# Strided products of an attention kernel: which side of the multiplication takes the stride

## The chip, the cores and the metric

The kernel runs on one core of a Trainium2 chip. Its time is the device time of the whole program in microseconds (us), the median of several executions; lower is better. Beside the times there is a profile of one execution: every instruction of every engine with its start and duration.

The engines that matter here are TensorE (PE, matrix products into PSUM), VectorE (DVE, element by element), ScalarE (ACT, activation functions and copies) and the queues of GpSimd (POOL) and SyncE (SP), which issue the transfers. PSUM is the memory that TensorE writes, in eight banks; SBUF is the main memory on the chip. Both have 128 partitions, and an instruction runs over the same elements of many partitions at once.

## The reference

Sparse attention with 8 batches, 8 heads, 576 positions and 64 columns a head, then a layer with a squared ReLU:

```python
scores = scale * np.matmul(q, k.transpose(0, 1, 3, 2))
mask_local = (rel >= 0) & (rel < 32)
mask_strided = (rel >= 0) & (pos[None, :] % 32 == pos[:, None] % 32)
# heads 0 to 3: mask_local; heads 4 to 7: mask_strided; masked scores are -1e9
attn = softmax(scores)                     # float32, over the keys
x = concatenated heads of attn @ v         # (8 * 576, 512)
h = np.maximum(x @ w_in, 0.0)              # w_in (512, 2048)
out = (h * h) @ w_out                      # w_out (2048, 512)
```

In a head with the strided mask a position sees only positions with the same remainder modulo 32: 18 of the 576. The kernel keeps x transposed, as four tiles xt[0] to xt[3] of 128 partitions (two heads of 64 columns each) and 4608 columns (all positions of all batches), in bf16. The strided heads 4 to 7 are xt[2] and xt[3]. The 18 positions of one remainder stand 32 columns, 64 bytes, apart there.

## The kernel before

The order of all work is written out by hand. The layer runs in nine chunks of 512 positions. A chunk is 16 groups of mm1 (four matmuls against w_in, L744, one for each xt tile in the order 0 to 3; then a ReLU on ScalarE, L750, into one of four r buffers, and a square on VectorE, L754) and 16 groups of mm2 (four matmuls against w_out, L850). Only chunk 0 takes the xt tiles in another order (0, 2, 1, 3). The groups are numbered from 0, so chunk c starts at group 32 c. The last two chunks (SEVEN) use a scheme with seven products for mm2 (L820), for which VectorE prepares sums of weights (L775).

A table, PLAN, says which steps of the attention of later batches go in front of which group; BATCH0 orders the first batch before the first group. Each engine works through its instructions in this order, and waits where an operand isn't there or a buffer isn't free. Batch b has positions 576 b to 576 b + 575, so chunk 1 needs batch 1, chunk 2 batch 2, and so on; chunk 7 needs batches 6 and 7.

The strided heads of a batch from 1 on are done by step_SS (scores and exponentials) and step_XX (words x1.0, x1.1, x1.2 for the three parts of batch 1). They pack three heads of one remainder into a block of 3 x 18 = 54 columns, two remainders (par 0 and 1) on the lower and upper 64 partitions. A part has eight blocks; the third part has six, which hold the fourth head. In step_XX TensorE makes the sums of the exponentials (L622, bank pn) and the products with v (L625, bank po); ScalarE makes the reciprocal of the sums, rv, with a logarithm and an exponential (L627, L628); and VectorE multiplies po by rv into xt: L635 for the first two parts, six instructions of 144 elements each (8 blocks by 18 positions), and L641 for the third, for each par one of 270 elements (three groups of 5 blocks by 18) and one of 18 elements. The last L641 of a batch completes xt[3].

Batch 0 uses step_N and step_O with another layout: VectorE multiplies 576 elements at once on all 128 partitions (L672), once for xt[2] and once for xt[3].

PSUM banks go round in a list: after group 32 six banks rotate among step_SS, step_XX, the local heads' steps and step_G. step_G(b) makes the scores of all local heads of batch b (L587, 24 matmuls) and takes six banks at once; its 24 matmuls alternate between two rows of three banks, eight matmuls to each pair of banks.

Of the kernel before, what the change touches and what calls it, by code (L numbers as in the profile page):

```python
# [11 lines left out]
ALU = mybir.AluOpType  # L12
# [155 lines left out]
def kernel(  # L168
# [9 lines left out]
    nc = tc.nc  # L178
    B, H, S, D = q.shape
    d_model, d_ff = moe_w_in.shape  # L180
    T = B * S
    STRIDE = 32
    NA = S // STRIDE
# [3 lines left out]
    NJ = 8  # L187
    RH = STRIDE // NJ
    SP_ = RH * NA
# [4 lines left out]
    NG = 5  # L194
    NB = NP2 + NG + 1
    W3 = 3 * NA
# [27 lines left out]
    def bank(nm):  # L224
        if places:
            return all_banks[places.pop(0)]
        t = banks[nm].pop(0)
        banks[nm].append(t)
        while id(t) in unread:
            run_due(lambda x: x[1] == unread[id(t)])  # L230
        return t

    def bank_pair():

        i = places.pop(0)
        return all_banks[i:i + 2], psb[:, i:i + 2]
# [21 lines left out]
    xt = [singles.tile([128, T], BF16, name=f"xt{p}") for p in range(4)]  # L258
# [10 lines left out]
    rv0 = b0[:, n_s:n_s + 8 * S].bitcast(FP32).rearrange("p (u c) -> p u c", u=4)  # L269
# [204 lines left out]
    def run_due(test):  # L474
        due = [x for x in pending if test(x)]
        for x in due:
            pending.remove(x)
        for x in sorted(due, key=lambda x: x[0]):
            x[2]()
# [121 lines left out]
    def blocks(part):  # L601
        return range(NJ * part, min(NJ * (part + 1), NB))
# [14 lines left out]
    def step_XX(b, part):  # L617
        run_due(lambda x: x[1] == (b, part))
        vb, n = vbds[b % 2], len(blocks(part))
        e = es[2 + b % 2][:, NJ * W3 * part:NJ * W3 * part + W3 * n]  # L620
        pn, po = bank("pt")[:, 0:W3 * n], bank("pt")
        nc.tensor.matmul(pn, ones_bd, e, start=True, stop=True)  # L622
        for i, t in enumerate(blocks(part)):
            c = slice(W3 * i, W3 * (i + 1))
            nc.tensor.matmul(po[:, c], vb[:, t, :], e[:, c], start=True, stop=True)  # L625
        rv = rv_pool.tile([128, NJ * W3], FP32, name="rv")[:, 0:W3 * n]
        nc.scalar.activation(rv, pn, AF.Ln)  # L627
        nc.scalar.activation(rv, rv, AF.Exp, scale=-1.0)  # L628
        for h in (3,) if part == 2 else range(3):
            for par in range(2):  # L630
                r, x = slice(64 * par, 64 * par + 64), slice(64 * (h % 2), 64 * (h % 2) + 64)
                to = xt[2 + h // 2][x, b * S:(b + 1) * S].rearrange("c (m a r) -> c m a r", a=NP2, r=2)
                if part < 2:
                    of, by = (y[r, 0:W3 * n].rearrange("c (a h m) -> c h m a", a=n, h=3)[:, h] for y in (po, rv))
                    nc.vector.tensor_tensor(to[:, :, NJ * part:NJ * (part + 1), par], of, by, op=ALU.mult)  # L635
                    continue
                of, by = (y[r, 0:W3 * n].rearrange("c (a g m) -> c g m a", a=n, g=3) for y in (po, rv))
                for lo, g, k in ((0, 0, NG), (NG, 2, 1)):
                    t = to[:, :, 2 * NG * (g == 2) + lo, par]
                    t = bass.AP(t.tensor, t.offset, [t.ap[0], [2 * NG, 3 - g], [STRIDE, NA], [2, k]])  # L640
                    nc.vector.tensor_tensor(t, of[:, g:, :, lo:lo + k], by[:, g:, :, lo:lo + k], op=ALU.mult)  # L641

    def load_v0():
        load_v_local_sw(0)
# [17 lines left out]
    def step_O(u):  # L662
        s = st.pop(u)
        e, hw, w = s["e"], S // 2, SP_
        pos, both = bank_pair()
        for half, po in enumerate(pos):
            for t in range(hw // w):
                for h in range(2):
                    vt, c = vs0[:, u - 2, NJ * h + 2 * t + half], ER * half + hw * h + w * t
                    nc.tensor.matmul(po[64 * h:64 * h + 64, w * t:w * (t + 1)], vt, e[0:w, c:c + w],  # L670
                                     start=True, stop=True)
        nc.vector.tensor_tensor(  # L672
            xt[u][:, 0:S].rearrange("c (p j r) -> c p j r", j=NJ // 2, r=2),
            both[:, :, 0:hw].rearrange("c r (j p) -> c p j r", p=SP_),
            rv0[:, u].rearrange("c (r j p) -> c p j r", r=2, p=SP_), op=ALU.mult)

    def step_D0(u):
        s = st[u]
# [196 lines left out]
    def run_step(word):  # L875
# [18 lines left out]
        elif op == "N":  # L894
            step_N(int(arg))
        elif op == "O":
            step_O(int(arg))
        elif op in "sx":
            (step_SS if op == "s" else step_XX)(*(int(x) for x in arg.split(".")))
        elif op == "k":  # L900
            step_K(int(arg[0]), int(arg[1]), ENG[arg[2]])
# [145 lines left out]
    for line in PLAN.strip().splitlines():  # L1047
        n, words = line.split(":")
# [42 lines left out]
```

## Time and profile before

| | us |
|---|---|
| median of 3 runs | 301.19 |
| lowest and highest run | 297.56, 304.58 |
| the profiled execution | 296.99 |
| its span, first to last instruction | 295.2 |
| TensorE busy | 289.3 |
| VectorE busy | 220.0 |
| ScalarE busy | 170.7 |
| GpSimd busy | 82.7 |

A row of a group reads: line, engine, operation, output <- inputs, partitions x elements and type of the output <- of the inputs, xcount | busy us in total, mean ns of one | idle us of the engine just before them, and what ended most of it. A row of the chain that ended last reads: start us, us, engine, tile and line, count. A row of the timeline is the same with shapes, and in brackets the idle time before it and what ended it. A row of waits reads: who <- whom: us in total, times, longest us. L635 is line 635 of the kernel.

### The profile page before, as it was taken

How to read it: one execution, taken by the hardware profiler on the slowest of the kernel's cores; microseconds unless marked ns; L12 is line 12 of the kernel's file. 1: busy time of each engine (PE TensorE's matmuls, PEld its weight loads, DVE VectorE, ACT ScalarE, POOL GpSimd, SP SyncE). 2: the span in 40 equal slices, each digit the busy share in tenths (PEclk: the TensorE clock that was granted, in tenths of full speed). 3: DMA queues.
4: the chain of work that ended last, by engine and by line, in shares of the span. 5: the costliest groups of instructions: out<-in, count | busy, mean ns of one | idle time of the engine just before them, and what ended most of it. 6: DMA issues, size and time to landing. Idle time of an engine off the chain costs nothing.

```text
span 295.2 us, 5930 instructions
## 1 busy us (share of the span) xinstructions
PE 289.3 (98%) x2212; PEld 156.1 (53%) x2212; DVE 220.0 (75%) x553; ACT 170.7 (58%) x321; POOL 82.7 (28%) x123
## 2 busy tenths in 40 slices
PE   8989999999999999999999999999999999999995
PEld 3644555545545454554455445544454444894594
DVE  5657689697777759679367945786489989968983
ACT  3758846775668736774577447645665466307610
POOL 8974743004513054075104800000000013102300
PEclk9999999999999999999999999999999999999999
DMA  7999999999999899999988999411011110021003
GB/s 159 176 208 205 192 198 192 155 216 207 174 194 171 144 157 202 160 136 181 167 131 122 179 168 145 84 56 73 36 23 52 58 54 0 1 104 41 0 2 142
DMA packets 91724, 37.38 MB, mean 127 GB/s; under 512 B 77548, under 2 KB 85830, under 8 KB 91696
## 3 DMA queue, kind: packets, MB, share of 16 engines
q0 software_dynamic: 50608, 18.33, 55.6%
q1 hardware_dynamic: 40944, 18.62, 31.8%
q8 instruction: 17, 0.28, 0.4%
q14 instruction: 11, 0.09, 0.1%
q10 hardware_dynamic: 144, 0.07, 0.1%
HBM read 37.22 MB, written 9.44 MB: 158 GB/s over the span
## 4 chain that ended last, share of the span: by engine, by line
PE 97%; DVE 1%; ACT 0%; issue 0%; DVEq 0%
PE psb L744 42%; PE psb L850 33%; PE psb L820 9%; PE psb L703 2%; PE psb L867 2%; PE psb L625 1%; PE psb L611 1%; PE psb L490 1%; PE psb L542 1%; PE psb L622 1%; PE psb L587 1%; PE psb L512 1%; DVE xt L672 0%; PE psb L347 0%; PE psb L337 0%; DVE x_l L692 0%
## 5 line engine op out<-in xcount | busy, mean ns | idle before, releaser
L744 PE MATMUL psb<-xt,w_in_b 128*128 128x512 bf16 x576 | 133.4, 379 | 0.3 <-DVE xt L672 0.2
L750 ACT ACTIVATE r<-psb 128x512 bf16<-128x512 f32 x144 | 85.4, 599 | 47.6 <-PE psb L744 42.5
L850 PE MATMUL psb<-w_out_b,g_sb 128*128 128x512 bf16 x448 | 103.2, 379 | 0.0
L744 PEld LDWEIGHTS <-w_in_b 128*128 128x128 bf16 x576 | 53.1, 97 | 58.7 <-issue 1.4
L754 DVE TENSOR_TENSOR g_sb<-r 128x512 bf16<-128x512 bf16 x112 | 46.9, 423 | 34.9 <-ACT r L750 34.0
L850 PEld LDWEIGHTS <-g_sb 128*128 128x128 bf16 x448 | 41.0, 97 | 44.7 <-DVE g_sb L754 0.3
L635 DVE TENSOR_TENSOR xt<-psb,rv 64x144 bf16<-64x144 f32 x84 | 34.0, 405 | 10.1 <-ACT rv L628 9.0
L789 POOL CAST sa<-g_sb 128x256 fp32r<-128x256 bf16 x16 | 9.7, 608 | 100.9 <-DVE g_sb L784 100.9
L854 ACT COPY y<-psb 128x512 f32<-128x512 f32 x28 | 16.6, 591 | 29.4 <-PE psb L850 29.3
L627 ACT ACTIVATE rv<-psb 128x432 f32<-128x432 f32 (+1 forms) x21 | 10.5, 501 | 12.8 <-PE psb L622 12.8
L365 POOL DMA_DIRECT2D q_t<-in_q_dram x6 | 3.5, 578 | 45.9 <-DMA qT_s<-q_t 26.2
L709 DVE TENSOR_TENSOR x_l<-psb,rinv 96x384 bf16<-96x384 f32 x28 | 15.5, 554 | 1.0
L784 DVE TENSOR_TENSOR g_sb<-r 128x512 bf16<-128x512 bf16 x32 | 13.1, 420 | 2.4 <-ACT r L750 2.4
L598 ACT ACTIVATE e<-psb 128x384 bf16<-128x384 f32 x30 | 12.0, 513 | 4.2 <-PE psb L587 4.2
L612 ACT ACTIVATE e<-psb 128x432 bf16<-128x432 f32 (+1 forms) x21 | 10.4, 497 | 4.0 <-PE psb L611 4.0
L294 POOL DMA_DIRECT2D k_l<-in_k_dram x16 | 11.8, 742 | 1.8 <-DMA v_st<-in_v_dram 1.3
L820 PE MATMUL psb<-t,s 128*128 128x256 f32 x96 | 12.2, 283 | 0.0
L594 DVE TENSOR_TENSOR e<-e,mask_all 128x576 bf16<-128x576 bf16 x20 | 8.4, 456 | 5.1 <-ACT e L598 5.0
L641 DVE TENSOR_TENSOR xt<-psb,rv 64x270 bf16<-64x270 f32 (+1 forms) x28 | 11.0, 432 | 1.4 <-ACT rv L628 1.1
L294 POOL DMA_DIRECT2D q_l<-in_q_dram x16 | 11.6, 730 | 0.5 <-DMA k_l<-in_k_dram 0.5
L820 PEld LDWEIGHTS psb<-t,s 128*128 128x128 f32 x96 | 11.6, 189 | 0.0
L628 ACT ACTIVATE rv<-rv 128x432 f32<-128x432 f32 (+1 forms) x21 | 11.2, 533 | 0.7
(135 smaller groups left out, 313.5 us busy)
## 6 DMA issues: line engine op xcount, KB each, us to landing
out_dram<-y SPq DMA_DIRECT2D x35, 256.0 KB, 3.3
w_out_b<-in_moe_w_out_dram POOLq DMA_DIRECT2D x4, 512.0 KB, 15.4
q_t<-in_q_dram POOLq DMA_DIRECT2D x7, 288.0 KB, 7.2
k_t<-in_k_dram POOLq DMA_DIRECT2D x7, 288.0 KB, 6.8
vl<-in_v_dram POOLq DMA_DIRECT2D x6, 288.0 KB, 6.6
v_st<-in_v_dram POOLq DMA_DIRECT2D x7, 216.0 KB, 6.8
w_in_b<-in_moe_w_in_dram POOLq DMA_DIRECT2D x2, 704.0 KB, 13.9
k_l<-in_k_dram POOLq DMA_DIRECT2D x16, 72.0 KB, 7.4
```

What stands on the lines that cost most here:

```text
L294: nc.gpsimd.dma_start(out=t[:, :, hh, :], in_=src[b, 2 * p + hh].rearrange("(t p) d -> p t d", p=QL))
L598: nc.scalar.activation(e[:, row, 4 * QL * i:4 * QL * (i + 1)], bk[row][i][:, 0:4 * QL], AF.Exp, scale=scale)
L628: nc.scalar.activation(rv, rv, AF.Exp, scale=-1.0)
L635: nc.vector.tensor_tensor(to[:, :, NJ * part:NJ * (part + 1), par], of, by, op=ALU.mult)
L709: nc.vector.tensor_tensor(x, po[0:QL, :, 0:D], rinv[0:QL].to_broadcast([QL, NL, D]), op=ALU.mult)
L744: nc.tensor.matmul(ph, w_in_b[:, kk, 128 * ff:128 * (ff + 1)], xt[kk][:, 512 * c:512 * (c + 1)], start=(kk == order[0]), stop=(kk == order ...
L750: nc.scalar.activation(r, ph, AF.Relu)
L754: later(1, lambda: nc.vector.tensor_tensor(g[:, ff, :], r, r, op=ALU.mult))
L784: nc.vector.tensor_tensor(g[:, ff, :], r, r, op=ALU.mult)
L820: nc.tensor.matmul(pa, a, b, start=k == 0 and n not in "273", stop=k == 7, skip_group_check=True)
L850: nc.tensor.matmul(py, g[:, ff, 128 * j:128 * (j + 1)], w_out_b[:, ff, :], start=(ff == 0), stop=(ff == 15))
L854: nc.scalar.copy(y, py)
```

## The change

All three products multiply two operands that lie packed (the positions of one remainder are neighbours) into an output in which they are apart. An instruction walks its operands and its output in one common order. Before, the order is that of the output: the inner loop goes over neighbouring remainders in xt and steps through both inputs by 54 floats (L635, L641), or by 72 and by half a buffer (L672). After, the order is that of the inputs: the inner loop goes over 18 (or 72) neighbours in po and rv, and steps through xt by 32 columns (L635, L641) or by 8 (L672). The elements, their number, the types, the instructions and their places in the order stay.

```diff
@@ step_XX
                 if part < 2:
-                    of, by = (y[r, 0:W3 * n].rearrange("c (a h m) -> c h m a", a=n, h=3)[:, h] for y in (po, rv))
-                    nc.vector.tensor_tensor(to[:, :, NJ * part:NJ * (part + 1), par], of, by, op=ALU.mult)
+                    of, by = (y[r, 0:W3 * n].rearrange("c (a h m) -> c h a m", a=n, h=3)[:, h] for y in (po, rv))
+                    t = to[:, :, NJ * part:NJ * (part + 1), par].rearrange("c m a -> c a m")
+                    nc.vector.tensor_tensor(t, of, by, op=ALU.mult)
                     continue
-                of, by = (y[r, 0:W3 * n].rearrange("c (a g m) -> c g m a", a=n, g=3) for y in (po, rv))
+                of, by = (y[r, 0:W3 * n].rearrange("c (a g m) -> c g a m", a=n, g=3) for y in (po, rv))
                 for lo, g, k in ((0, 0, NG), (NG, 2, 1)):
                     t = to[:, :, 2 * NG * (g == 2) + lo, par]
-                    t = bass.AP(t.tensor, t.offset, [t.ap[0], [2 * NG, 3 - g], [STRIDE, NA], [2, k]])
-                    nc.vector.tensor_tensor(t, of[:, g:, :, lo:lo + k], by[:, g:, :, lo:lo + k], op=ALU.mult)
+                    t = bass.AP(t.tensor, t.offset, [t.ap[0], [2 * NG, 3 - g], [2, k], [STRIDE, NA]])
+                    nc.vector.tensor_tensor(t, of[:, g:, lo:lo + k], by[:, g:, lo:lo + k], op=ALU.mult)
@@ step_O
         nc.vector.tensor_tensor(
-            xt[u][:, 0:S].rearrange("c (p j r) -> c p j r", j=NJ // 2, r=2),
-            both[:, :, 0:hw].rearrange("c r (j p) -> c p j r", p=SP_),
-            rv0[:, u].rearrange("c (r j p) -> c p j r", r=2, p=SP_), op=ALU.mult)
+            xt[u][:, 0:S].rearrange("c (p j r) -> c r j p", j=NJ // 2, r=2),
+            both[:, :, 0:hw].rearrange("c r (j p) -> c r j p", p=SP_),
+            rv0[:, u].rearrange("c (r j p) -> c r j p", r=2, p=SP_), op=ALU.mult)
```

## The prediction

> **What bounds the kernel now.** I read, in this order: the page's busy times and the chain that ended last, the list of what TensorE waited for, the groups of VectorE by shape, and then the timeline of VectorE beside the chain, batch by batch.
>
> ```profile
> PE 289.3 (98%) x2212; PEld 156.1 (53%) x2212; DVE 220.0 (75%) x553; ACT 170.7 (58%) x321; POOL 82.7 (28%) x123
> ...
> PE 97%; DVE 1%; ACT 0%; issue 0%; DVEq 0%
> ```
> ```profile
> PE psb L867 <- DVE xt L976: 1.3, 1, 1.3
> PE psb L725 <- DVE x_l L692: 0.5, 1, 0.5
> PE psb L744 <- DVE xt L672: 0.2, 1, 0.2
> ```
>
> TensorE is busy 289.3 of 295.2 us and holds 97% of the chain; its list of waits has these three entries and no more, and one of them, 0.2 us, is for a changed line. So a faster VectorE can give back next to nothing. A slower one costs whatever passes the slack that stands before TensorE's next use. The question has two halves: what one changed product costs, and how much slack each has.
>
> **What one product costs.** The groups of VectorE by shape, and below them the durations of L641 with its two forms mixed (shortest/median/longest):
>
> ```profile
> L635 DVE TENSOR_TENSOR xt<-psb,rv 64x144 bf16<-64x144 f32 x84 | 34.0, 405 | 10.1 <-ACT rv L628 9.0
> L641 DVE TENSOR_TENSOR xt<-psb,rv 64x270 bf16<-64x270 f32 x14 | 8.9, 635 | 1.4 <-ACT rv L628 1.1
> L832 DVE TENSOR_TENSOR y<-psb,y 128x256 f32<-128x256 f32 x19 | 8.1, 424 | 4.3 <-PE psb L820 3.5 <-issue 0.7
> L641 DVE TENSOR_TENSOR xt<-psb,rv 64x18 bf16<-64x18 f32 x14 | 3.2, 229 | 0.0
> L672 DVE TENSOR_TENSOR xt<-psb,g_sb 128x576 bf16<-128x576 f32 x2 | 2.3, 1164 | 1.5 <-PE psb L670 1.4
> L829 DVE TENSOR_TENSOR y<-psb,y 128x128 f32<-128x128 f32 x2 | 0.5, 286 | 0.5 <-PE psb L820 0.5
> ```
> ```profile
> L641 DVE TENSOR_TENSOR xt<-psb,rv x28: 220/433/649, 49.8 to 236.7; 64x270 bf16<-64x270 f32 x14, 64x18 bf16<-64x18 f32 x14
> ```
>
> L832 and L829 are products of the same kind of operands (one from PSUM, one from SBUF) with everything in order: 424 and 286 ns for 256 and 128 elements, so 1.08 ns an element over a fixed 148. The changed forms all read with a long step today, and with the same 148 they take 1.78 ns an element (L635: 257/144), 1.80 (L641: 487/270) and 1.76 (L672: 1016/576), although they write in three different ways: pairs of bytes 4 B apart in runs of 8, the same in runs of 5, and without gaps. So today the reading sets the rate, and the change takes that away.
>
> What it puts in its place is in the trace once. The small form of L641 (18 elements) has one column, so it already reads 18 neighbours and writes each 64 B from the last, as every L635 and L641 will. At 1.08 ns it would take 167 ns. It takes 229 in the mean and 220 at the least: (229-148)/18 = 4.5, (220-148)/18 = 4.0 ns for an element. That it is so short leaves room for doubt, since a fixed 50 ns would look the same.
>
> The other row with single strided writes is the memset L982 (48 elements, 144 B apart), from the timeline of VectorE:
>
> ```profile
> 1.55 0.10 DVE L982 MEMSET vl<- 128x48 bf16 x1
> 1.81 0.49 DVE L983 MEMSET vl<- 32x520 bf16 x1 [0.17 <-DVE vl L982]
> ...
> 7.38 0.30 DVE L948 COPY mask_all<-mask_loc 128x576 bf16<-128x576 bf16 x1
> 7.75 0.10 DVE L949 MEMSET mask_all<- 32x48 uint32 x1
> ```
>
> It lasts 0.10 us, as long as the dense memset of 48 (L949): by duration a strided write is free. But what waits for it starts 0.26 us after its start, while L949 starts 0.07 us after the end of the copy it waits for; on that pattern L983 would have come at 0.17. The 0.09 us over it, spread on 48 elements and added to a memset's own 0.8 ns (0.39 us more for the 472 elements more of L983), make 2.7 ns.
>
> So a strided element costs between 1.08 (the dense rows) and 4.5 ns. I take 4.2, between the two readings of the 18-element form, because that form is the changed form itself: same engine, same operands, same step. Then:
> - L635: 148 + 144 x 4.2 = 753, 348 ns more, 84 times: 29.2 us.
> - L641, large form: 148 + 270 x 4.2 = 1282, 647 ns more, 14 times: 9.1 us. Its small form stays.
> - L672: steps of 16 B, which no row shows; 148 + 576 x (1.08 to 4.5) is 770 to 2740. By the nearest row 2567: 1.40 us more, twice.
>
> VectorE's work grows by 41 us to 261. No instruction, wait or transfer is added or moved: each engine's order is that of before, only shapes turn (18x8 becomes 8x18). Nothing on SP or POOL passes anything.
>
> **Where the slack ends.** One batch has twelve L635 and two large L641: 12 x 0.348 + 2 x 0.647 = 5.47 us more; six L635 alone are 2.09. What waits for them: at the chunks 1, 2 and 7 the fourth matmul of the first group (L744) reads xt[3], which the last L641 writes. At chunks 3 to 6 step_G (L587) comes first: it takes all six rotating banks, the same as the three parts of step_XX before it, so its 18th matmul needs the bank that the last L641 reads (for batch 3's first part, the 17th and the sixth L635). VectorE's second L672 and its last pieces of each batch, and then TensorE's pieces of the chain:
>
> ```profile
> 19.23 1.15 DVE L672 TENSOR_TENSOR xt<-psb,g_sb 128x576 bf16<-128x576 f32 x1 [1.35 <-PE psb L670]
> ...
> 49.78 1.58 DVE L641 TENSOR_TENSOR xt<-psb,rv 64x270 bf16<-64x270 f32 x4
> ...
> 81.71 1.58 DVE L641 TENSOR_TENSOR xt<-psb,rv 64x270 bf16<-64x270 f32 x4
> ...
> 95.44 2.49 DVE L635 TENSOR_TENSOR xt<-psb,rv 64x144 bf16<-64x144 f32 x6 [0.59 <-ACT rv L628]
> ...
> 111.25 1.57 DVE L641 TENSOR_TENSOR xt<-psb,rv 64x270 bf16<-64x270 f32 x4
> ...
> 139.01 1.58 DVE L641 TENSOR_TENSOR xt<-psb,rv 64x270 bf16<-64x270 f32 x4
> ...
> 168.10 1.56 DVE L641 TENSOR_TENSOR xt<-psb,rv 64x270 bf16<-64x270 f32 x4
> ...
> 196.46 2.50 DVE L635 TENSOR_TENSOR xt<-psb,rv 64x144 bf16<-64x144 f32 x6 [0.59 <-ACT rv L628]
> 200.09 1.59 DVE L641 TENSOR_TENSOR xt<-psb,rv 64x270 bf16<-64x270 f32 x4 [1.12 <-ACT rv L628]
> ...
> 235.31 1.59 DVE L641 TENSOR_TENSOR xt<-psb,rv 64x270 bf16<-64x270 f32 x4
> ```
> ```profile
> 1.26 4.02 PE psb L867 x9
> ...
> 16.69 1.19 DVE xt L672
> 17.93 0.81 PE psb L744 x3
> 19.11 9.17 PE psb L744 x42
> ...
> 51.61 0.86 PE psb L744 x4
> ...
> 83.85 6.91 PE psb L744 x32
> ...
> 98.69 0.62 PE psb L587 x24
> ...
> 112.92 0.61 PE psb L587 x24
> ...
> 140.29 0.68 PE psb L587 x24
> ...
> 171.09 0.62 PE psb L587 x24
> ...
> 203.55 0.62 PE psb L587 x24
> ...
> 237.73 13.81 PE psb L744 x64
> ```
>
> The end of the VectorE work, the time at which TensorE uses it (start plus three matmuls of 0.216, from 32 in 6.91, or plus 17/24 or 16/24 of the L587 piece), and growth minus slack:
> - chunk 1: 51.36, used 52.26, slack 0.90: waits 4.57. Chunk 2: 83.29, 84.50, 1.21: 4.26.
> - batch 3, first part: 97.93, 99.10, 1.17, growth 2.09: 0.92. Rest: 112.82, 113.35, 0.53, growth 2.09 + 1.29 = 3.38: 2.85.
> - batch 4: 140.59, 140.77, 0.18: 5.29. Batch 5: 169.66, 171.53, 1.87: 3.60.
> - batch 6: idle gaps of 0.59 and 1.12 take up a part, 2.09 - 0.59 + 2.09 - 1.12 + 1.29 = 3.76; 201.68, 203.99, 2.31: 1.45.
> - chunk 7: 236.90, 238.38, 1.48: 3.99.
> - prologue: TensorE already waits for the first L672, so all 1.40; the second starts at 19.23 and ends at 20.38, its use is nine matmuls into the x42 piece, 21.07: 1.40 - 0.69 = 0.71.
>
> The sum is 26.9 + 2.1 = 29.0 us. Each wait stands alone, for VectorE catches up while TensorE runs the next chunk. What the backlog does to the squares (L754) queued behind the products I cost at nothing: most products fall into stretches of L850, which uses squares made before. Without that cover a batch's 5.47 us would hold back L750's four r buffers instead, in place of the waits above, not on top of them.
>
> The profiled execution took 296.99 us (span 295.2): 296.99 + 29.0 = **326 us**. It lies under the median of the runs shown, 301.19, and under the lowest, 297.56; the runs' spread of 7 us is why I take 2%, 6 us, as what a measurement of this kernel can tell from no change. With 4.0 ns the same list gives 25.7 us and 322.6; with 4.5, 34.2 and 331.2.
>
> **Rivals.**
> - *A half price.* The memset's 2.7 ns hold: L635 537, L641 877, L672 1703 ns; a batch grows 2.06 us, and the list leaves 1.16 + 0.85 + 0.74 + 1.88 + 0.19 + 0.58 + 0.54 = 5.9 us: 303. For it the late L983; against it the 18-element form.
> - *A strided write costs what a strided read costs.* At 1.76 to 1.80 ns nothing changes: 297. For it, every strided read here has this one rate, whatever its step; against it, 18 elements would then take 180 ns, and not one took under 220.
>  The Trainium skill (SBUF — State Buffer, Specifications) says of SBUF that lines are 16 bytes and each cross to a new line pays a penalty, with no word that a write pays more than a read. By that rule old and new form cross as often, and the sum would be 297. The trace agrees for the reads, not for the 18-element form.
> - *Not slower: strided writes are free.* The engine hands a write on and takes the next element, as the memset's 0.10 us would have it. L635 falls to 148 + 144 x 1.08 = 304, L641 to 440, L672 to 770. TensorE gets only the 0.2 us it waits for L672: 296.8. The sign turns where an element costs less than 1.78 ns.
> - *TensorE comes back slow.* The granted clock by slices:
>
> ```profile
> PEclk9999999999999999999999999999999999999999
> ```
>
>  It stands at 0.9 or more throughout, the start included; yet the nine matmuls of L867 at the start take 0.447 us each, those of chunk 2 0.216. If the four waits of about 4 us or more (4.57, 4.26, 5.29, 3.99) each bring such a start back, 4.02 us at that pace lose 2.1: 8.3 us more, 334. No idle of that length stands in the middle of this trace, so nothing speaks for or against.
>  The Trainium skill (TensorE: Matmul & The Clock Gate, Part 1) puts the clock at half after about 3.4 us of idling; no run here shows it yet.
>
> That the change does not do what it says is out: the shapes turn in the order of the instructions.
>
> **How the numbers follow.** Forecast 0.50, half price 0.12, equal price 0.17, free 0.13, slow TensorE 0.08. Slower by over 2%: forecast, slow TensorE and half of the half price, 0.64. Within 2%: 0.35. Faster by over 2%: 0.01, since TensorE's 289.3 us stay. The range must take in the equal price below and the slow TensorE above: 297 to 334. The forecast's own range is 315 to 332.
>
> **What would show it.** In the profile after: L635 near 750 ns, L641's large form near 1280, L672 near 2570, its small form still near 229; TensorE's waits list L744 and L587 behind VectorE, 4 to 5 us each, the longest in front of step_G of batch 4. L635 near 305 or 405 refutes the price; L635 near 750 without these waits refutes the slack. Wrong too if L672's 16 B step is priced apart from 64 B, though that moves only 2 us.

## The result

The changed kernel takes 344.0 us (median of 4 runs, 340.61 to 344.73) against 299.38 for the kernel before: slower by a ratio of 1.150, 95% interval 1.135 to 1.164. The forecast was 326 with a range of 297 to 334: the direction is right, the size is not. The ratios compare the fast executions alone: some executions of a kernel run 1.5% or more longer than its fastest, so a median and a ratio do not always give quite the same time. The profiled execution has a span of 342.9 us, 47.7 more than before.

The page of the changed kernel (busy times, granted clock by slices, chain). Its lines from step_XX on stand one number higher: L636, L642, L673, L745, L755 and L851 are the L635, L641, L672, L744, L754 and L850 of before.

```profile
PE 300.7 (88%) x2177; PEld 159.0 (46%) x2212; DVE 266.2 (78%) x553; ACT 172.1 (50%) x321; POOL 82.8 (24%) x123
...
PEclk9999999899989998799879996999999998999999
...
PE 61%; DVE 28%; issue 5%; ACT 3%; DMA 2%; POOL 0%; DVEq 0%; POOLq 0%
```

Two things have changed. TensorE, once on 97% of the chain, is on 61%, and VectorE on 28%: TensorE's idle time grew from 295.2 - 289.3 = 5.9 to 42.2 us. And TensorE's own busy time grew by 11.4 us, though it does the same work; the granted clock has slices at 0.6 to 0.8 where it had none. 36.3 + 11.4 make the 47.7. The split is a rough one. This trace holds 2177 of the 2212 matmuls, and where a record is missing a short gap counts as idle: 31 gaps of 0.05 us and three of 0.3, some 2.7 us, belong to the second part, which is then about 14 us. (The last run below, nearly the same kernel with all 2212 on record, has 305.3 us busy and 36.5 idle.)

The groups of VectorE by shape, changed kernel:

```profile
L636 DVE TENSOR_TENSOR xt<-psb,rv 64x144 bf16<-64x144 f32 x84 | 66.1, 787 | 9.9 <-ACT rv L628 8.8
...
L642 DVE TENSOR_TENSOR xt<-psb,rv 64x270 bf16<-64x270 f32 x14 | 18.6, 1327 | 0.3
...
L642 DVE TENSOR_TENSOR xt<-psb,rv 64x18 bf16<-64x18 f32 x14 | 6.1, 437 | 0.0
L673 DVE TENSOR_TENSOR xt<-psb,g_sb 128x576 bf16<-128x576 f32 x2 | 5.4, 2724 | 1.5 <-PE psb L671 1.4
```

Over the fixed 148 ns, an element takes 4.44 (L636), 4.37 (L642) and 4.47 ns (L673), the upper of the two readings of the 18-element form. That form itself is unchanged and yet went from 229 to 437 ns: its record now begins 0.36 us before that of the large form in front of it ends (98.43 and 98.79 us in batch 2; 0.08 us in the kernel before). Two pairs take 2.82 us together (the chain has 1.40 and 1.42 for a pair), as 1.33 us + 18 x 4.4 ns for each would.

What TensorE waited for, changed kernel (us in total, times, longest):

```profile
PE psb L745 <- DVE xt L642: 12.2, 3, 4.7
PE psb L587 <- DVE xt L642: 7.4, 3, 2.5
PE psb L587 <- DVE xt L636: 5.7, 4, 3.0
PE psb L745 <- DVE xt L673: 2.6, 2, 1.7
PE psb L851 <- DVE g_sb L755: 2.1, 1, 2.1
PE psb L622 <- DVE xt L636: 1.7, 1, 1.7
```

These six entries are 31.7 us. Taken one by one from the timeline of TensorE, beside the prediction's list:

| where | forecast | measured |
|---|---|---|
| prologue, two L673 (the first: 1.73 less the 0.18 of before) | 1.40 + 0.71 | 1.55 + 0.83 |
| chunk 1 | 4.57 | 1.71 (L622) + 3.13 (L745) |
| chunk 2 | 4.26 | 4.65 |
| batch 3, first part, then the rest | 0.92, 2.85 | 1.13, 2.50 |
| batch 4 | 5.29 | 2.97 + 2.42 |
| batch 5 | 3.60 | 1.30 + 2.51 |
| batch 6 | 1.45 | 2.08, on a square (L755) and not on step_G |
| chunk 7 | 3.99 | 4.41 |
| sum | 29.0 | 31.2 |

What the list lacks comes after the waits. Stretches of the changed kernel (columns: stretch, us, then busy us and instruction count of PE, PEld, DVE, ACT, POOL, then the granted clock, DMA share, GB/s): the wait in front of chunk 2, the 4 us behind it, and the 4 us behind those.

```profile
95.70:100.30 4.60, 0.00 (x0) 0.00 (x0) 4.54 (x7) 0.00 (x0) 0.55 (x2) 1.00 1.21 209
100.30:104.30 4.00, 3.95 (x11) 1.47 (x11) 2.98 (x5) 1.32 (x3) 2.54 (x4) 0.57 1.11 200
104.30:108.30 4.00, 3.95 (x20) 1.77 (x19) 2.73 (x9) 2.86 (x5) 0.00 (x0) 1.00 1.90 139
```

Behind the wait TensorE is busy throughout, but starts 11 matmuls in 4 us instead of 20, at a granted clock of 0.57. In the kernel before the same matmuls ran with 21 in 4 us:

```profile
83.80:87.80 4.00, 4.00 (x21) 1.77 (x19) 2.48 (x6) 2.83 (x5) 0.63 (x2) 1.00 1.35 217
```

### The profile page after: what moved, and what is told of

It reads as the page before. It is cut to its first block, busy times and chain, and to the rows that moved or that the text cites. A ratio compares the mean times of both kernels' runs of the same rounds, so it can differ in the third digit from the quotient of the medians.

```text
span 342.9 us, 5895 instructions
## 1 busy us (share of the span) xinstructions
PE 300.7 (88%) x2177; PEld 159.0 (46%) x2212; DVE 266.2 (78%) x553; ACT 172.1 (50%) x321; POOL 82.8 (24%) x123
## 4 chain that ended last, share of the span: by engine, by line
PE 61%; DVE 28%; issue 5%; ACT 3%; DMA 2%; POOL 0%; DVEq 0%; POOLq 0%
PE psb L745 33%; DVE xt L636 15%; PE psb L851 14%; PE psb L821 8%; DVE xt L642 5%; DVE t L776 2%; DMA w_out_b<-in_k_dram 2%; DVE xt L673 2%; PE psb L704 1%; DVE g_sb L755 1%; PE psb L611 1%; DVE q_l L313 1%; ACT rv L628 1%; ACT rv L627 1%; PE psb L542 1%
## 5 line engine op out<-in xcount | busy, mean ns | idle before, releaser
L745 PE MATMUL psb<-xt,w_in_b 128*128 128x512 bf16 x557 | 138.0, 391 | 15.8 <-DVE xt L642 12.2
L851 PE MATMUL psb<-w_out_b,g_sb 128*128 128x512 bf16 x432 | 106.2, 393 | 3.7 <-DVE g_sb L755 2.1
L745 PEld LDWEIGHTS <-w_in_b 128*128 128x128 bf16 x576 | 54.6, 100 | 74.7 <-issue 21.0
L755 DVE TENSOR_TENSOR g_sb<-r 128x512 bf16<-128x512 bf16 x112 | 46.9, 422 | 42.1 <-ACT r L751 41.4
L636 DVE TENSOR_TENSOR xt<-psb,rv 64x144 bf16<-64x144 f32 x84 | 66.1, 787 | 9.9 <-ACT rv L628 8.8
L851 PEld LDWEIGHTS <-g_sb 128*128 128x128 bf16 x448 | 42.3, 100 | 51.1 <-issue 6.8
L598 ACT ACTIVATE e<-psb 128x384 bf16<-128x384 f32 x30 | 12.7, 504 | 15.9 <-PE psb L587 15.9
L642 DVE TENSOR_TENSOR xt<-psb,rv 64x270 bf16<-64x270 f32 (+1 forms) x28 | 19.7, 882 | 0.3
L587 PE MATMUL psb<-qT,kTl 64*128 64x96 bf16 x120 | 5.2, 217 | 13.2 <-DVE xt L642 7.4
L427 POOL DMA_DIRECT2D v_st<-in_v_dram x7 | 3.9, 559 | 37.4 <-DVE vb L434 34.1
```

The lines of the kernel that those rows point to most:

```text
L636: nc.vector.tensor_tensor(t, of, by, op=ALU.mult)
L642: nc.vector.tensor_tensor(t, of[:, g:, lo:lo + k], by[:, g:, lo:lo + k], op=ALU.mult)
L745: nc.tensor.matmul(ph, w_in_b[:, kk, 128 * ff:128 * (ff + 1)], xt[kk][:, 512 * c:512 * (c + 1)], start=(kk == order[0]), stop=(kk == order ...
L755: later(1, lambda: nc.vector.tensor_tensor(g[:, ff, :], r, r, op=ALU.mult))
L851: nc.tensor.matmul(py, g[:, ff, 128 * j:128 * (j + 1)], w_out_b[:, ff, :], start=(ff == 0), stop=(ff == 15))
```

## Experiments

The kernel before ran at 297.2 to 297.4 us (median) beside them. "Idle" is TensorE's, span less busy time.

**Only L635, or everything but L672.** The first takes the hunk of L635 alone, the second leaves out that of L672:

```diff
-                    of, by = (y[r, 0:W3 * n].rearrange("c (a h m) -> c h m a", a=n, h=3)[:, h] for y in (po, rv))
+                    of, by = (y[r, 0:W3 * n].rearrange("c (a h m) -> c h a m", a=n, h=3)[:, h] for y in (po, rv))
...
```

> Only L635 (84 products of 144) reads in order; L641 and L672 as before. Theory (VectorE's longer products use up the slack before TensorE's next use, and the waits then bring a slow TensorE clock): L635 at 787 ns, 382 more each, 4.58 us a batch; growth minus slack gives waits of 3.7 and 3.4 at chunks 1 and 2, 1.1 and 1.8 at batch 3, 4.4, 2.7, 0.6 and 3.1 at batches 4 to 6 and chunk 7, in all 21 us, so a profiled time near 318 without a slow clock and up to 324 with it. Rival (the waits are few and the strided writes slow the other engines through the memory): the waits on L635 stay well under 15 us, and the matmuls' time to the next one grows although the granted clock stays at 1.0.

> The changed kernel with L672 as before, L635 and L641 reading in order. Theory: the first chunk's mm1 ends as in the kernel before (33.7 us instead of 37.9), for the waits of 2.6 us on L672 go, and with them a shift that brought two copies of L313 under a GpSimd memset (1.50 and 1.73 us instead of 0.35). From there on nothing changes: 340, 4 us under the changed kernel. Rival (the long copies have another cause, such as the strided writes themselves): the copies of L313 stay long, and the time is 341 to 342.

L635 alone: 327.26 us, ratio 1.097 (1.090 to 1.103); 1.097 times the 297.4 of before is 326 us, 2 above the 324 expected at most. Its page:

```profile
PE 293.7 (91%) x2177; PEld 157.3 (48%) x2212; DVE 250.8 (77%) x553; ACT 172.2 (53%) x321; POOL 82.9 (26%) x123
...
PEclk9999999799989999999899999999999999999999
```

Idle 324.3 - 293.7 = 30.6, 24.7 us more than before, and 4.4 us of slower matmuls (35 records are missing here too, and in the next two pages). The growth is that of TensorE's waits on VectorE, and the slower matmuls come with the granted clock down in three slices, so the rival falls on both counts.

Without L672: 340.16 us, ratio 1.145 (1.142 to 1.147), as expected. Here and in the run with L635 alone the long copies are gone. In the changed kernel they stand like this (timeline of VectorE, then of GpSimd):

```profile
30.50 1.50 DVE L313 COPY q_l<-xt 96x768 bf16<-96x768 bf16 x1
...
32.85 1.73 DVE L313 COPY q_l<-xt 96x768 bf16<-96x768 bf16 x1
```
```profile
30.51 1.27 POOL L970 MEMSET vb<- 128x1408 f32 x1
...
33.07 1.29 POOL L970 MEMSET kb<- 128x1408 f32 x1
```

Each copy starts beside a memset and ends after it; it takes 0.35 us elsewhere.

**The same time on VectorE without strided writes.** Every L635 is issued twice, in its old form:

```diff
+                    for _ in range(2):
-                    nc.vector.tensor_tensor(to[:, :, NJ * part:NJ * (part + 1), par], of, by, op=ALU.mult)
+                        nc.vector.tensor_tensor(to[:, :, NJ * part:NJ * (part + 1), par], of, by, op=ALU.mult)
```

> The kernel before, with every L635 issued twice in its old form (strided reads, writes in runs 4 B apart), so that VectorE gets 419 ns more for each of the 84 without one strided write of the new kind. Theory (only the time of VectorE's queue counts): growth 5.0 us a batch, waits of 24 us in all, and the slow clock behind the longer ones: 321 to 329, some 3 us above the run with L635 alone changed. Rival (strided writes burden the memory for other engines): no such burden here, so it stays clearly below the run with L635 alone changed, under 318.

334.84 us, ratio 1.125 (1.122 to 1.129): by the ratios some 8 us above L635 alone, not below it. The rival is out: old-form products that fill the queue equally cost no less. But it is also above the theory's 321 to 329. Its page shows where:

```profile
PE 301.3 (90%) x2177; PEld 159.5 (48%) x2212; DVE 253.2 (76%) x637; ACT 172.0 (52%) x321; POOL 83.5 (25%) x123
...
PEclk9999997999959997999699987999999997999999
```

Idle is 333.9 - 301.3 = 32.6 us, 2.0 more than with L635 alone; the other 7.6 us are slower matmuls. Waits that differ by little left TensorE slow for much longer. So the clock's part is large and jumps; I had sized it as a small supplement. The next experiment shows where the jumps come from.

**TensorE kept busy.** The changed kernel with matmuls of no use ahead of the waits, so that the time passes in work:

```diff
+        if ff == 0 and c in (1, 2, 7):
+            busy(ph, 14 if c == 1 else 18)
         for kk in kks:
...
+        busy(bk[0], {3: 4, 4: 10, 5: 12, 6: 12, 7: 0}[b])
         bk = [bk[0::2], bk[1::2]]
...
+    def busy(ps, n):
+        for _ in range(n):
+            nc.tensor.matmul(ps, w_in_b[:, 0, 0:128], w_in_b[:, 0, 0:512], start=True, stop=True)
```

> The changed kernel with matmuls of no use ahead of the waits: 14, 18 and 18 before the first group of chunks 1, 2 and 7, and 4, 10, 12 and 12 before step_G of batches 3 to 6's waits, each as long as 0.216 us, into a bank that the next real matmul overwrites. They fill time in which TensorE would wait. Theory (TensorE's clock falls to half behind waits of some us): the granted clock stays near 1.0, chunk 1's, 2's and 3's mm1 after the wait run at 0.216 us a matmul, and the time falls by about 11 us to 333. Rival (matmuls are slower for another reason, contention with the strided writes): the clock in the records or the pace does not recover, and the time stays at 344 or rises by what the added matmuls take.

334.66 us, where about 333 was expected: 88 matmuls more, and 9.3 us less than the changed kernel, at the same length of VectorE's work. The stretch behind the wait of chunk 2, in this kernel, runs at full pace again:

```profile
99.70:103.70 4.00, 4.00 (x19) 1.85 (x19) 3.52 (x8) 2.53 (x5) 2.69 (x3) 1.00 1.15 175
```

The mean granted clock is 0.990 instead of 0.955. That settles the second part of the loss: the slow matmuls come from TensorE's idling, not from traffic of the strided writes.

How much idling it takes can be read from the traces of these kernels, stretch by stretch. The clock on record is 1.00 or 0.50 and nothing between (0.57 was a mean over both), and within a trace it changes only at points that lie 3.41 us or a multiple of it apart. Behind the wait of chunk 2 in the changed kernel it is at half from 100.45 to 103.86 us; in all it is at half for 30.7 us, in six pieces of 3.41 or 6.83, and TensorE is busy in some 24 of them, so that about 12 us are lost (an estimate, half of the 24). With L635 alone it is at half for 10.2 us, with L635 twice for 30.7, in this kernel for 6.8. Take the stretches of 3.41 us from one such point to the next that ran at full clock, in the changed kernel and in all its variants here but the one with single products (the last 5 us of each left out). Behind 31 of the 33 with 1.72 us or more of idling the clock went to half, and behind none with less than 1.70. So it matters how a wait lies to these points. With L672 alone a wait of 1.73 us fell into one stretch, and the clock went down (first fence); with L635 alone the wait of 3.16 us in front of chunk 7 was cut into 1.46 and 1.70 us, and it did not (second fence):

```profile
17.77:21.18 3.41, 1.68 (x22) 0.74 (x21) 2.06 (x2) 0.82 (x2) 2.25 (x3) 1.00 1.18 210
21.18:24.59 3.41, 3.41 (x9) 1.21 (x8) 2.48 (x1) 0.00 (x0) 0.76 (x1) 0.50 1.23 207
```
```profile
262.19:265.60 3.41, 1.90 (x9) 0.78 (x8) 3.38 (x6) 1.13 (x3) 0.00 (x0) 1.00 0.19 74
265.60:269.02 3.42, 1.72 (x8) 0.78 (x8) 3.36 (x8) 1.04 (x2) 0.00 (x0) 1.00 0.01 4
269.02:272.43 3.41, 3.41 (x17) 1.57 (x16) 3.27 (x9) 2.35 (x5) 1.31 (x2) 1.00 0.02 5
```

**What one strided element costs, alone.** Behind the kernel before, products of 64x144 with both inputs in order, when nothing else runs; four of each.

```diff
+    four = [(slice(64 * p, 64 * p + 64), slice(64 * h, 64 * h + 64)) for h in range(2) for p in range(2)]
+    n, bk = 8 * 18, psb[:, 5]
+    for r, x in four:
+        nc.vector.tensor_tensor(x16[x, 0:32 * n:32], bk[r, 0:n], src[r, 0:n], op=ALU.mult)
...
```

> The kernel before, followed by products of 64x144 (one operand from PSUM, one from SBUF, both in order) whose output step is 2, 4, 8, 16, 32, 64 and 48 B in bf16, 4 and 64 B in f32, pairs of neighbours 64 B apart, and runs of 8 at 4 B; then the same product with one input alone read in the old long step; 18 and 72 elements; a memset and a copy on ScalarE, dense and at 64 B. Nothing else runs on the chip by then. Theory (a price for each 16 B line that a write enters): about 300 ns at 2 and 4 B and in runs of 8, 460 at 8 B (two to a line) and in pairs, 780 at 16, 32, 48 and 64 B, in f32 at 64 B too; 18 elements 167 dense and 225 at 64 B, 72 elements 460. Rival (memory banks: only steps of 64 B meet one bank): 48 B well under 64 B. Rival (two-byte writes pay): f32 at 64 B near 300. Rival (other engines' traffic makes the price): 64 B well under 780 here, where the engines idle. Of the old form, the input from SBUF read with the long step makes 405, that from PSUM no more than 300 (a copy from PSUM with a 192 B step took 1.0 ns an element).

The groups of VectorE and ScalarE in this kernel (the columns as before; mean ns is the number after the busy us):

```profile
L1081 DVE TENSOR_TENSOR xt<-psb,y 64x144 bf16<-64x144 f32 x4 | 3.3, 815 | 0.1
L1075 DVE TENSOR_TENSOR xt<-psb,y 64x144 bf16<-64x144 f32 x4 | 3.2, 792 | 0.1
L1079 DVE TENSOR_TENSOR xt<-psb,y 64x144 bf16<-64x144 f32 x4 | 3.1, 780 | 0.1
L1077 DVE TENSOR_TENSOR xt<-psb,y 64x144 bf16<-64x144 f32 x4 | 3.0, 756 | 0.1
L1073 DVE TENSOR_TENSOR xt<-psb,y 64x144 bf16<-64x144 f32 x4 | 1.9, 474 | 0.1
L1103 DVE TENSOR_TENSOR xt<-psb,y 64x72 bf16<-64x72 f32 x4 | 1.9, 468 | 0.1
L1085 DVE TENSOR_TENSOR xt<-psb,y 64x144 f32<-64x144 f32 x4 | 1.6, 396 | 0.1
L1096 DVE TENSOR_TENSOR xt<-psb,y 64x144 bf16<-64x144 f32 x4 | 1.6, 394 | 0.1
L1071 DVE TENSOR_TENSOR xt<-psb,y 64x144 bf16<-64x144 f32 x4 | 1.3, 318 | 0.1
...
L1087 DVE TENSOR_TENSOR xt<-psb,y 64x144 bf16<-64x144 f32 x4 | 1.2, 306 | 0.1
L1093 DVE TENSOR_TENSOR xt<-psb,y 64x144 bf16<-64x144 f32 x4 | 1.2, 305 | 0.1
L1069 DVE TENSOR_TENSOR xt<-psb,y 64x144 bf16<-64x144 f32 x4 | 1.2, 305 | 0.1
...
L1101 DVE TENSOR_TENSOR xt<-psb,y 64x18 bf16<-64x18 f32 x4 | 0.9, 234 | 0.1
L1107 DVE MEMSET xt<- 64x144 bf16 x4 | 0.7, 178 | 2.2 <-DVE xt L1107 1.1 <-issue 1.1
L1099 DVE TENSOR_TENSOR xt<-psb,y 64x18 bf16<-64x18 f32 x4 | 0.7, 174 | 0.1
```
```profile
L1111 ACT CAST xt<-psb 64x144 bf16<-64x144 f32 x4 | 3.1, 777 | 0.1
...
L1109 ACT CAST xt<-psb 64x144 bf16<-64x144 f32 x4 | 1.1, 274 | 43.4 <-DVE xt L1107 43.3
```

| output | line | ns | | output or input | line | ns |
|---|---|---|---|---|---|---|
| dense | L1069 | 305 | | pairs, 64 B apart | L1087 | 306 |
| 4 B | L1071 | 318 | | f32, 64 B | L1085 | 396 |
| 8 B | L1073 | 474 | | 18 elements, dense / 64 B | L1099, L1101 | 174, 234 |
| 16 B | L1075 | 792 | | 72 elements, 64 B | L1103 | 468 |
| 32 B | L1077 | 756 | | long step in the PSUM input only | L1093 | 305 |
| 48 B | L1081 | 815 | | long step in the SBUF input only | L1096 | 394 |
| 64 B | L1079 | 780 | | ScalarE, dense / 64 B | L1109, L1111 | 274, 777 |
| f32, dense | L1083 | 305 | | runs of 8 at 4 B | L1090 | 308 |

- For lone two-byte writes the price is one of each 16 B line: 474 with two elements to a line (72 lines), and from 16 to 64 B, where each element enters its own, all within 756 to 815. 48 B is no cheaper than 64, so it is not banks that only steps of 64 B would meet; and 780 on an idle chip is near the 787 of L636 in the changed kernel, so it is not other traffic.
- It is the price of a write of two bytes: in f32 the same 64 B step costs 396, that is (396 - 148)/144 = 1.7 ns an element instead of 4.4, and pairs of bf16 neighbours, 64 B apart, take 306, like the dense form, although they enter as many lines as the step of 8 B with its 474. Of my three rivals this one holds in part; my own expectation of 780 for f32 and 460 for pairs was wrong. What in the hardware makes a lone two-byte write dearer is not shown.
- 18, 72 and 144 elements (234, 468, 780) lie on a line of about 4.3 ns an element over 156. So the 229 ns of the kernel before were a price for each element, and no fixed 50 ns.
- The old form's 405 come from its SBUF input: 394 with the long step there alone, 305 with it in the PSUM input alone.
- The memset at 64 B is recorded with 178 ns, but 2.2 us of idle time stand before the four, 0.55 in front of each, the first one too. With it one takes 0.74 us from start to start, near the 144 x 4.4 = 634 ns and a fixed part. The record holds only the last piece; the writes lie in the idle time in front of it. So the 0.10 us of L982 in the kernel before did not say that its writes were free. The 2.7 ns that I worked out from the wait behind it have no support here either: the timeline of VectorE, then of ScalarE, shows that the record is the end, for the copy that waits for this memset starts 0.03 us after it. What the 0.17 us behind L982 were stays open.

```profile
326.18 0.18 DVE L1107 MEMSET xt<- 64x144 bf16 x1 [0.56 <-DVE xt L1107]
```
```profile
326.39 0.58 ACT L1109 CAST xt<-psb 64x144 bf16<-64x144 f32 x2 [42.41 <-DVE xt L1107]
```

**L672 alone and L641 alone.** Each takes its hunk of the diff, nothing else.

> Only L672 (two products of 576 with a 16 B step) reads in order. Theory: 2724 ns each, TensorE waits 1.7 and 0.8 us for them, so 2.4 us more at the first chunk; and if the shift brings the copies of L313 under a GpSimd memset, as in the changed kernel, some 2 us more: 299.5 to 302. Rival (the prologue's other waits hide it): 297.4.

> Only L641 reads in order. Theory: the large form 1327 ns, 1.4 us more a batch; minus slack 0.5 at chunk 1, 0.2 at chunk 2, 0.9 at batch 3 and 1.2 at batch 4, none elsewhere, none long enough for a slow clock: 300.2. So the three parts alone add about 30 (L635), 3 (L672) and 3 (L641) us, less than the 44 to 46 of the whole, for slack is spent once and the clock falls only behind long waits. Rival (the parts add up): L641 alone gives 10 us or more.

L672 alone: 303.23 us, ratio 1.015 (1.005 to 1.026); 1.015 times the 297.2 of before is 301.7 us, within what was expected, though the interval is wide. L641 alone: 300.61, ratio 1.013 (1.008 to 1.017), as expected, with a mean granted clock of 1.00. TensorE's waits in the two, L641 first:

```profile
PE psb L587 <- DVE xt L641: 1.9, 2, 1.1
...
PE psb L744 <- DVE xt L641: 0.5, 1, 0.5
```
```profile
PE psb L744 <- DVE xt L672: 1.7, 1, 1.7
...
PE psb L490 <- DVE k_l L313: 1.1, 2, 0.9
PE psb L490 <- DVE q_l L313: 0.8, 1, 0.8
```

With L672 alone TensorE also waits 1.9 us for copies of L313, and the granted clock has early slices at 0.8. By the ratios the three parts alone add 9.7, 1.5 and 1.3%: 12.5 of the 15.0% of the whole.

**The memsets moved away from the copies**, in the changed kernel:

```diff
-6: o2 l2k8+9 mv0g o3 mk0g
+6: o2 l2k8+9 o3
-14: W1q0v T5qa
+14: W1q0v T5qa mv0g
-16: W1q1v T5ka
+16: W1q1v T5ka mk0g
```

> The changed kernel with GpSimd's two memsets of 1408 elements (words mv0g and mk0g) moved from group 6 to groups 14 and 16. Theory (a copy in SBUF on VectorE stands still while GpSimd writes a memset; the 2.6 us that L673 adds brought two copies of L313 under them): every L313 at 0.35 to 0.4 us, the first chunk's mm1 2 us shorter, 341 to 342. Rival (the copies are long for another reason): they stay at 1.5 us or more, 344.

```profile
L313 DVE COPY q_l<-xt 96x768 bf16<-96x768 bf16 x7 | 2.4, 348 | 0.0
```

The copies are short, so the memsets were their cause. The time is not: 343.75 us, ratio 1.156 (1.153 to 1.159). The profile of this run has a slice at 0.8 of the clock in the first chunk, where that of the changed kernel has none, and the first mm1 is only 0.6 us shorter. That slice is one more stretch of 3.41 us at half clock, behind the wait for the first L673, which in this trace falls whole into one stretch and in the changed kernel's is cut in two; it takes back up to 1.7 us (an estimate, half of 3.41). What the copies cost the changed kernel in time stays open.

## Why the prediction was wrong

- **The price of an element** was taken as 4.2 ns and measured 4.4 to 4.5. The working from the 18-element form was right, and so was its mean (4.5); I went below it because a fixed part could not be excluded, which the 72 and 144 elements now do. L635 was put at 753 and is 787, L641 at 1282 (1327), L672 at 2567 (2724); VectorE's total at 261 and is 266 (2.6 of it the two long copies). With 4.5 my own list gave 331. The 16 B step of L672, for which no row stood, costs like 64 B.
- **The slack** was right almost place by place: 29.0 us forecast, 31.2 measured (with the measured durations the same list gives 32.8), with the most in front of batch 4's step_G, 5.4 us, though in two pieces. The squares that I costed at nothing did hold TensorE once, 2.1 us before batch 6's step_G, in place of the wait there.
- **The step that failed** is "TensorE comes back slow". I made it a rival with a chance of 0.08, priced at 8.3 us on top of 4.2 ns, and let 334 close the range. It happened, and cost 11.4 us of TensorE's busy time by the page, some 14 with the missing records. That it came together with the upper price makes 331 + 11.4 = 342.6, near the 344.0 of the run, but this is in part luck: the list at 4.5 ns has 34.2 us of waits where 31.2 were measured, and other pieces fill the gap. The slow clock was no alternative to the forecast but a consequence of the waits that the forecast contained, and belonged into the sum. Also, I asked for waits of about 4 us. It came behind the four that I named, and behind the 2.5 us of batch 3 and the 1.3 + 2.5 us of batch 5 as well. In the changed kernel the clock is down behind waits of 2.5 to 3 us too:

```profile
165.60:173.00 7.40, 1.68 (x18) 0.95 (x18) 6.61 (x10) 2.08 (x5) 0.00 (x0) 0.71 0.83 132
173.00:177.00 4.00, 4.00 (x14) 1.60 (x13) 1.33 (x3) 1.12 (x3) 0.00 (x0) 0.68 0.02 6
```

 That is the stretch of batch 4's two waits and the 4 us behind it. The Trainium skill (TensorE: Matmul & The Clock Gate, Part 1) has the clock at half after about 3.4 us without work; 11 matmuls in place of 20 agree with the half. The time does not agree: the runs show the fall behind 1.73 us of idling (L672 alone), and it went by whether about half of a stretch of 3.41 us was idle.
- **The rivals.** Half price, equal price and free writes are all out. What spoke for "free", the memset's duration, was a misread row, and the 2.7 ns worked out from what waited for it fit no product measured here at steps from 16 to 64 B. The Trainium skill's 16 B lines (SBUF — State Buffer, Specifications) were right in that the price rises up to a step of 16 B and no further. They did not hold for two elements to a line, to which that row of the Trainium skill grants full bandwidth: L1073 took 474 ns in place of 305. That a two-byte write pays two and a half times what a read pays is not in that rule, and it decided the case.
- **The rest** of the idling (36.3 us less the 31.2 listed) is about 5 us: some 2.7 are the gaps of missing records, and in the prologue TensorE waits 0.8 us for a copy under a memset (L490) and 0.7 for a transfer (L347). I had not seen that L672, by its 2.4 us, shifts VectorE against GpSimd.

## What to carry to other kernels

Where a VectorE product must take a stride on one side and its output has two bytes an element, leave the stride to the reads, or write neighbours in pairs: a lone two-byte write into each 16 B line took 4.4 ns an element, a strided read from SBUF 1.7, one from PSUM nothing. When TensorE is at 98%, price a slower engine by each place's slack, and add a slow clock behind the waits, as part of the sum and not as a separate case. Here it cost up to 1.7 us for each 3.41 us at half clock; a wait of 1.73 us brought it where it fell into one such stretch, one of 3.16 us that was cut in two did not, and all waits above 3.2 us did. A form that occurs once in the profile, however small, is better evidence for its price than a rule.

## What the runs showed of the hardware

- A strided write costs by 16 B lines entered and by the width written: 4.4 ns for two bytes alone, 1.7 for four; pairs of bf16 neighbours took no longer than the dense form (306 and 305 ns). It is not VectorE's own: ScalarE's copy goes from 274 to 777 ns with the same step.
- The record of the 18-element form behind the large strided one lasted 437 ns instead of 229; it began 0.36 us before its predecessor's record ended.
- The record of a strided memset (178 ns) is only its end; about 0.55 us of it show as idle time in front.
- Two copies in SBUF on VectorE took 1.50 and 1.73 us instead of 0.35 beside memsets of 1.3 us on GpSimd.
- The granted clock of TensorE was 1.00 or 0.50, in pieces of 3.41 us or multiples of it. It went to half behind 31 of 33 stretches of 3.41 us with 1.72 us or more of idling and behind none with less than 1.70. Nearly equal VectorE load (250.8 and 253.2 us) gave 10.2 or 30.7 us at half clock, and 293.7 or 301.3 us of TensorE's busy time.
